# Weights times values on quarters of the array: two partial sums in two banks, one pair of heads a step

## The chip, the cores and the metric

The kernel runs on one core of one Trainium2 chip. The metric is the device time of one execution in microseconds (us). The core has TensorE (PE; its weight loads are shown apart as PEld), VectorE (DVE), ScalarE (ACT), GpSimd (POOL) and SyncE (SP), each with its own queue, worked off in order; they wait for each other by semaphores. TensorE writes to PSUM, which has eight banks of 2 KB per partition.

## What is computed

Attention whose scores are mixed across the 12 heads before the softmax and whose weights are mixed across the heads after it, and behind it two expert layers, all in float32 (batch 2, 12 heads, 448 tokens, 64 per head):

```python
def _attn_ref(q, k, v, w_pre, w_post):
    scale = 1.0 / np.sqrt(q.shape[-1])
    scores = scale * np.matmul(q, k.transpose(0, 1, 3, 2))
    scores = np.einsum('bhij,hg->bgij', scores, w_pre)
    scores = scores - np.max(scores, axis=-1, keepdims=True)
    attn = np.exp(scores)
    attn = attn / (np.sum(attn, axis=-1, keepdims=True) + 1e-09)
    attn = np.einsum('bhij,hg->bgij', attn, w_post)
    return np.matmul(attn, v)
...
x = _moe_ref(x, w_gate, w_val, w_out)    # (silu(x wg) * (x wv)) wo
x = _moe2_ref(x, w_in, w_out)            # (h * relu6(h + 3) / 6) w2o with h = x w2i
```

## The kernel before

The 896 query tokens are cut into 8 tiles t of up to 120 tokens, four for each batch entry, and each tile into 9 to 12 chunks of 10 tokens (90 chunks). Two chunks make one step i of the main loop (45 steps); in the 128 partitions of a chunk lie heads times tokens, which makes the mix over heads a matmul.

For each pair of heads c of a tile, `scores` (L166, tile name pqk) multiplies queries and keys on quarters of the array (64 rows by 64 columns) into two banks, and `scores_out` (L182) copies them to S: the even head on VectorE, the odd one on ScalarE. `relayout` (SP) and `relayout_rest` (GpSimd, L206) move S by DMA into the order of chunks, sx. `premix` (L217, ppre) mixes the heads; `row_max` (L230, VectorE), `exps` (L236, ScalarE) and `weights` (L242 and L243 on VectorE, L245 on GpSimd, wn) prepare the softmax; the division goes into wn, a copy of w_post for each row. `postmix` (L259, ppost) multiplies with wn and brings the keys to the partitions. `attn_out` (L283) copies its two banks to the tile at: the first on VectorE, the second on ScalarE.

When a tile is complete, `av` (L295, pav) multiplies its weights with the values, a pair of heads c at a time, on 128 rows (keys) by 64 columns (one head each), in one bank. `x_out` (L313) copies that bank on VectorE to a staging tile xs, which `x_split` on GpSimd later splits into two float32r parts (xh, xl). For the last two tiles `x_last` (L333 ScalarE, L334 VectorE) does that straight from the bank.

The order of a step i is written out by hand. TensorE: postmix(i), scores of the pairs due in that step, premix(i + 2), in the last three steps some matmuls of the first expert product (`fill`), then av of the pairs due. ScalarE: the exponentials for step i + 1, the second bank of attn_out, the second score copy. VectorE: the first bank of attn_out, the reciprocals of the first chunk of step i + 1, the first score copy, the reciprocals of the second chunk, two maxima, then x_out. Tables give each pair its step: a tile's scores lie in the steps ahead of its first premix (those of tiles 2 to 7 end in steps 7, 13, 17, 24, 29 and 35), and av of tile t lies behind the tile's last postmix, two pairs in each of three steps. The expert weights of the first two products are converted in steps 24 to 27 and 32 to 35.

The PSUM tags are pqk (2 banks; scores and av), ppre (4) and ppost (2). Behind step 44 and the rest of `fill`, av of tile 7 runs for all six pairs with ppre and ppost in turn, and then the expert products, which take TensorE to the end.

## Time and profile before

| | us |
|---|---|
| median of three runs | 717.46 (711.99 to 725.30) |
| the profiled execution | 713.29 |
| its span, first to last instruction | 711.5 |
| TensorE, MATMUL records | 685.4 (96%) |
| VectorE | 503.4 (71%) |
| ScalarE | 296.9 (42%) |
| GpSimd | 176.5 (25%) |

Busy times come from one profiled execution. The ends of matmuls are modelled, so records overlap and a busy TensorE is not one at its peak; how long a block takes is read from its start to the next block's start. A float32 matmul shows as two records.

### The profile page before, as it was taken

How to read it: one execution, taken by the hardware profiler on the slowest of the kernel's cores; microseconds unless marked ns; L12 is line 12 of the kernel's file. 1: busy time of each engine (PE TensorE's matmuls, PEld its weight loads, DVE VectorE, ACT ScalarE, POOL GpSimd, SP SyncE). 2: the span in 40 equal slices, each digit the busy share in tenths (PEclk: the TensorE clock that was granted, in tenths of full speed). 3: DMA queues.
4: the chain of work that ended last, by engine and by line, in shares of the span. 5: the costliest groups of instructions: out<-in, count | busy, mean ns of one | idle time of the engine just before them, and what ended most of it. 6: DMA issues, size and time to landing. Idle time of an engine off the chain costs nothing.

```text
span 711.5 us, 16611 instructions
## 1 busy us (share of the span) xinstructions
PE 685.4 (96%) x6864; PEld 571.6 (80%) x6864; DVE 503.4 (71%) x853; ACT 296.9 (42%) x563; POOL 176.5 (25%) x275
## 2 busy tenths in 40 slices
PE   9699899799899999999999999999999999999997
PEld 3355565465579999999999999999999999999997
DVE  4676677688745888888888665668888888765550
ACT  4565466456543433434343322334445544333320
POOL 2444265454640221131112000002332332000000
PEclk9999999899999999999999999999999999999999
DMA  5777456443421424323242334232323323544420
GB/s 198 225 204 202 134 138 180 136 145 84 132 92 46 134 89 133 121 101 130 93 131 92 119 106 132 89 92 92 127 89 96 127 82 100 162 145 145 136 72 27
DMA packets 33629, 86.75 MB, mean 122 GB/s; under 512 B 9264, under 2 KB 21952, under 8 KB 33552
## 3 DMA queue, kind: packets, MB, share of 16 engines
q1 hardware_dynamic: 25632, 80.97, 35.3%
q0 software_dynamic: 7200, 3.94, 2.8%
q8 instruction: 54, 0.88, 0.5%
q10 hardware_dynamic: 720, 0.77, 0.3%
q14 instruction: 23, 0.19, 0.1%
HBM read 62.20 MB, written 2.75 MB: 91 GB/s over the span
## 4 chain that ended last, share of the span: by engine, by line
PE 87%; DMA 5%; issue 2%; DVE 2%; ACT 2%; POOL 1%; SPq 0%; POOLq 0%; ACTq 0%
PE pi L394 16%; PE pp L394 16%; PE po L394 12%; PE pg L394 12%; PE pv L394 12%; PE ppost L259 5%; PE pav L295 5%; PE pqk L166 4%; PE ppre L217 3%; DMA sx<-S 3%; DMA k<-in_k_dram 1%; PE p L394 1%; ACT e L236 1%; DMA q<-in_q_dram 1%; POOL wn L245 1%
## 5 line engine op out<-in xcount | busy, mean ns | idle before, releaser
L394 PE MATMUL pp<-g,hp 128*128 128x448 f32 x384 | 109.1, 365 | 0.0
L605 POOL TENSOR_TENSOR g<-rl,g 128x448 fp32r<-128x448 f32 x32 | 41.5, 1318 | 168.5 <-ACT g L604 168.5
L394 PE MATMUL po<-u,ho 128*128 128x448 f32 x288 | 81.7, 364 | 0.0
L236 ACT ACTIVATE e<-ppre,nm 128x448 f32<-128x448 f32 x90 | 56.4, 631 | 52.8 <-DVE nm L230 52.7
L259 PEld LDWEIGHTS ppost<-wn,e 60*64 60x64 f32 x2880 | 49.5, 137 | 34.3 <-POOL wn L245 29.7
L394 PEld LDWEIGHTS pp<-g,hp 128*128 128x128 f32 x384 | 72.0, 187 | 5.8
L605 POOL TENSOR_TENSOR u<-sg,u 128x448 fp32r<-128x448 f32 x24 | 32.9, 1391 | 151.2 <-ACT u L604 151.2
L394 PE MATMUL pi<-x2h,li 128*128 128x448 f32 x192 | 70.2, 366 | 0.0
L394 PE MATMUL pi<-x2l,hi 128*128 128x448 f32 x192 | 70.0, 364 | 0.0
L394 PE MATMUL pi<-x2h,hi 128*128 128x448 f32 x192 | 69.9, 364 | 0.0
L394 PE MATMUL pp<-g,lp 128*128 128x448 f32 x192 | 69.3, 361 | 0.0
L259 PE MATMUL ppost<-wn,e 60*64 60x60 f32 x2880 | 56.1, 224 | 12.5 <-POOL wn L245 11.3
L206 POOL DMA_DIRECT2D sx<-S x90 | 54.5, 606 | 33.9 <-issue 11.0
L230 DVE TENSOR_REDUCE nm<-ppre 128x1 f32<-128x448 f32 x90 | 51.7, 613 | 12.7 <-PE ppre L217 12.0
L394 PEld LDWEIGHTS po<-u,ho 128*128 128x128 f32 x288 | 54.1, 188 | 3.8
L217 PE MATMUL ppre<-sx,W 64*64 64x448 f32 x360 | 51.1, 558 | 4.6 <-DMA sx<-S 4.6
L166 PE MATMUL pqk<-k,q 64*64 64x448 f32 (+4 forms) x384 | 51.5, 570 | 2.6 <-ACT S L182 2.0
L394 PE MATMUL po<-u,lo 128*128 128x448 f32 x144 | 52.3, 363 | 0.0
L394 PE MATMUL pg<-xl,hg 128*128 128x448 f32 x138 | 50.5, 366 | 0.0
L394 PE MATMUL pv<-xl,hv 128*128 128x448 f32 x138 | 50.5, 366 | 0.0
L394 PE MATMUL pg<-xh,hg 128*128 128x448 f32 x138 | 50.5, 366 | 0.0
L295 PEld LDWEIGHTS pav<-at,v 128*64 128x64 f32 x768 | 36.9, 137 | 16.9 <-ACT S L182 11.8
(105 smaller groups left out, 1369.3 us busy)
## 6 DMA issues: line engine op xcount, KB each, us to landing
sx<-S SPq DMA_DIRECT2D x90, 182.0 KB
ri<-in_moe_w_in_dram SPq DMA_DIRECT2D x16, 768.0 KB
rg<-in_moe_w_gate_dram SPq DMA_DIRECT2D x12, 768.0 KB
rv<-in_moe_w_val_dram SPq DMA_DIRECT2D x12, 768.0 KB
ro<-in_moe_w_out_dram SPq DMA_DIRECT2D x12, 768.0 KB
rp<-in_moe_w_out_dram SPq DMA_DIRECT2D x12, 640.0 KB
rp<-in_moe_w_out_dram SPq DMA_DIRECT2D x6, 768.0 KB
sx<-S POOLq DMA_DIRECT2D x90, 42.0 KB, 4.9
```

The source lines that it names most:

```text
L166: nc.tensor.matmul(p[e][lo:hi, :S], lhsT=qs[b][r, base + lo : base + hi], rhs=ks[b][r, c, :], start=True, stop=True, tile_position=(64 * e ...
L206: nc.gpsimd.dma_start(out=sx[m // 2][104:128, m % 2, :], in_=rows[8:, :H, :])
L217: nc.tensor.matmul(p[a][64 * r : 64 * r + 64, :S], lhsT=W1[rows, :], rhs=x[rows, r, :], start=True, stop=True, tile_position=(64 * a, 64 * r),
L230: nc.vector.tensor_reduce(nm, pre[m][:, :S], AX.X, ALU.max, negate=True)
L236: nc.scalar.activation(e[:, :S], pre.pop(m)[:, :S], AF.Exp, bias=tot.pop(m), scale=1.0, accum_out=sm)
L245: nc.gpsimd.tensor_scalar(wn, W2, rc, 1.0, ALU.mult, ALU.mult)
L259: nc.tensor.matmul(p[s][64 * c : 64 * c + 64, r, b, :, :], lhsT=e[rows, k0 : k0 + 64], rhs=wn[rows, :, :], start=True, stop=True, tile_pos ...
L295: nc.tensor.matmul(p[64 * e : 64 * e + 64, :n], lhsT=vs[b][:, jc, h, :], rhs=ats[t][:, jc, h, :n], start=jc == 0, stop=jc == JC - 1, tile_ ...
L394: nc.tensor.matmul(p[:, :S], lhsT=wt[:, kk, :], rhs=xx, start=start, stop=stop)
L605: eng.tensor_tensor(to[1], src, to[0].bitcast(F32), ALU.subtract)
```

## The change

`av` uses quarters of the array as scores, premix and postmix do. The 128 rows of keys are cut into two halves of 64; each half accumulates in a bank of its own (p[0] and p[1]), so that a pair of heads is 16 matmuls on 64 rows by 64 columns instead of 8 on 128 by 64. `add_halves` brings the two banks together on the way out: a ScalarE copy of the first, then a VectorE add of the second. In x_out this stands in the place of the VectorE copy; in x_last it is put ahead of the cast and the subtraction, with a new tile xl.

The table of steps is changed too: a tile's pairs are spread one to a step where the steps suffice (two in steps 18, 20, 23 and 40) instead of two in every second or third. `attn_out` is cut in two: its second bank, on ScalarE, is now copied behind the step's scores and score copies. From step 43 on av takes banks of ppre, and at the end each pair of tile 7 takes two banks of ppre or two of ppost.

```diff
-    def av(t, c, tag="pqk"):
+    def av(t, c, tags=("pqk", "pqk")):
...
-        p = ps.tile([128, 512], F32, name=f"pav{t}_{c}", tag=tag, bufs=BUFS[tag])
+        p = [ps.tile([128, 512], F32, name=f"pav{t}_{c}_{r}", tag=tags[r], bufs=BUFS[tags[r]]) for r in range(2)]
         for jc in range(JC):
-            for e in range(2):
-                h = 2 * c + e
-                nc.tensor.matmul(
-                    p[64 * e : 64 * e + 64, :n],
-                    lhsT=vs[b][:, jc, h, :],
-                    rhs=ats[t][:, jc, h, :n],
-                    start=jc == 0,
-                    stop=jc == JC - 1,
-                    tile_position=(0, 64 * e),
-                )
+            for r in range(2):
+                for e in range(2):
+                    h = 2 * c + e
+                    nc.tensor.matmul(
+                        p[r][64 * e : 64 * e + 64, :n],
+                        lhsT=vs[b][64 * r : 64 * r + 64, jc, h, :],
+                        rhs=ats[t][64 * r : 64 * r + 64, jc, h, :n],
+                        start=jc == 0,
+                        stop=jc == JC - 1,
+                        tile_position=(64 * r, 64 * e),
+                    )
...
-        nc.vector.tensor_copy(stage[t][:, c, :n], pavs.pop((t, c))[:, :n])
+        add_halves(stage[t][:, c, :n], pavs.pop((t, c)), n)
+
+    def add_halves(out, p, n):
+        nc.scalar.copy(out, p[0][:, :n])
+        nc.vector.tensor_tensor(out, out, p[1][:, :n], ALU.add)
...
-        p = pavs.pop((t, c))[:, :n]
+        x = pe.tile([128, 120], F32, name=f"xl{t}_{c}", tag="xl", bufs=4)
+        p = x[:, :n]
+        add_halves(p, pavs.pop((t, c)), n)
...
-            i = begin + (c // 2) * (end - begin) // 2
-            at_step(i, av, t, c, place="av")
+            i = begin + c * (end - begin + 1) // HP
+            at_step(i, av, t, c, ("pqk" if i < NP - 2 else "ppre",) * 2, place="av")
...
         if i >= 0:
-            attn_out(i)
+            attn_out(i, 0)
         for m in soft[:1]:
             weights(m)
         run(i, "qk")
+        if i >= 0:
+            attn_out(i, 1)
...
-        av(7, c, ("ppre", "ppost")[c % 2])
+        av(7, c, (("ppre", "ppre"), ("ppost", "ppost"))[c % 2])
```

In VectorE's order at the end of step 14 (tile 1's pairs 2 and 3 in the kernel before) stand, before:

```order
L230 TENSOR_REDUCE nm32_1495<-ppre16_0_1489 128x1
L230 TENSOR_REDUCE nm33_1497<-ppre16_1_1490 128x1
L313 COPY xs1_1334<-pav1_2_1499 128x120
L313 COPY xs1_1334<-pav1_3_1508 128x120
L283 COPY at2_1285<-ppost15_0_1528 128x2x48x5
```

and now:

```order
L230 TENSOR_REDUCE nm32_1575<-ppre16_0_1569 128x1
L230 TENSOR_REDUCE nm33_1577<-ppre16_1_1570 128x1
L316 TENSOR_TENSOR xs1_1394<-xs1_1394,pav1_2_1_1580 128x120
L281 COPY at2_1345<-ppost15_0_1608 128x2x48x5
L242 TENSOR_SCALAR rc32_1647<-sm32_1642 128x1
```

Two copies out of the banks of pairs 2 and 3 have become one add for pair 2, of its second bank (pav1_2_1); pair 3 has moved into step 15.

In ScalarE's order the exponentials for step 16 (e2, e3) and what follows them in step 15 stand, before:

```order
L236 ACTIVATE e2_113,sm32_1562<-ppre16_0_1489,nm32_1495 128x448
L236 ACTIVATE e3_114,sm33_1564<-ppre16_1_1490,nm33_1497 128x448
L283 COPY at2_1285<-ppost15_1_1529 128x2x48x5
L182 COPY S0_107<-pqk4_3_1_1574 110x448
L236 ACTIVATE e4_115,sm34_1635<-ppre17_0_1586,nm34_1592 128x448
```

and now:

```order
L315 COPY xs1_1394<-pav1_2_0_1579 128x120
L236 ACTIVATE e2_113,sm32_1642<-ppre16_0_1569,nm32_1575 128x448
L236 ACTIVATE e3_114,sm33_1644<-ppre16_1_1570,nm33_1577 128x448
L182 COPY S0_107<-pqk4_3_1_1653 110x448
L281 COPY at2_1345<-ppost15_1_1609 128x2x48x5
L315 COPY xs1_1394<-pav1_3_0_1676 128x120
L236 ACTIVATE e4_115,sm34_1735<-ppre17_0_1666,nm34_1672 128x448
```

The score copy stands ahead of the at copy now, and the copy of the pair's first bank stands ahead of the exponentials of the next step.

## Rows read from the trace of the kernel before

**Rows 1.** Busy us by stretch; columns: stretch, length, engines' busy (instructions), clock, DMA.

```profile
43.26:219.06 175.80, 161.29 (x3853) 102.81 (x3852) 118.81 (x354) 95.80 (x238) 84.46 (x173) 0.98 0.47 137
219.06:711.50 492.44, 488.72 (x2414) 452.61 (x2412) 359.72 (x433) 179.03 (x274) 74.42 (x56) 1.00 0.34 109
```

**Rows 2.** The same view, 43.26 to 219.06 cut; engines: PE, PEld, DVE, ACT, POOL.

```profile
43.26:55.17 11.91, 11.79 (x274) 6.47 (x273) 8.74 (x26) 7.17 (x18) 4.27 (x10) 1.00 0.65 186
55.17:65.04 9.87, 9.37 (x197) 4.94 (x193) 6.85 (x20) 4.90 (x12) 4.89 (x11) 1.00 0.66 195
65.04:75.84 10.80, 10.80 (x224) 6.19 (x224) 7.07 (x21) 5.80 (x15) 4.57 (x11) 1.00 0.79 198
75.84:98.28 22.44, 20.02 (x483) 11.56 (x481) 15.80 (x46) 12.91 (x33) 9.93 (x22) 1.00 0.36 118
98.28:121.56 23.28, 22.86 (x602) 14.95 (x600) 17.66 (x55) 13.90 (x36) 14.26 (x30) 1.00 0.68 190
121.56:165.19 43.63, 36.68 (x859) 21.98 (x857) 29.88 (x86) 24.08 (x57) 21.29 (x45) 0.92 0.46 135
165.19:188.30 23.11, 20.54 (x552) 12.93 (x553) 18.61 (x56) 13.49 (x33) 10.92 (x25) 1.00 0.32 93
188.30:219.06 30.76, 29.23 (x676) 23.78 (x676) 14.19 (x48) 13.56 (x37) 14.33 (x25) 1.00 0.25 85
```

**Rows 3.** TensorE in order of time: start, us, line, out<-in, [idle before <-releaser].

```profile
66.02 1.79 PE L166 MATMUL pqk<-k,q 64*64 64x448 f32 x8
67.74 0.98 PE L217 MATMUL ppre<-sx,W 64*64 64x448 f32 x8
...
101.91 1.16 PE L259 MATMUL ppost<-wn,e 60*64 60x60 f32 x64
102.89 0.93 PE L166 MATMUL pqk<-k,q 64*64 64x448 f32 x8
103.65 0.93 PE L217 MATMUL ppre<-sx,W 64*64 64x448 f32 x8
104.50 1.89 PE L295 MATMUL pav<-at,v 128*64 128x120 f32 x32
106.32 1.16 PE L259 MATMUL ppost<-wn,e 60*64 60x60 f32 x64
```

**Rows 4.** Groups by line and shape, 43.26 to 219.06: busy us, mean ns | idle before.

```profile
L230 DVE TENSOR_REDUCE nm<-ppre 128x1 f32<-128x448 f32 x76 | 43.7, 613 | 8.3 <-PE ppre L217 7.7
L283 DVE COPY at<-ppost 128x480 f32<-128x480 f32 x39 | 26.3, 675 | 19.9 <-PE ppost L259 19.8
L182 DVE COPY S<-pqk 120x448 f32<-120x448 f32 x14 | 8.5, 609 | 3.0 <-PE ppre L217 1.9 <-DMA sx<-S 0.6 <-PE pqk L166 0.5
L334 DVE TENSOR_TENSOR xl<-pav,xh 128x120 fp32r<-128x120 f32 x6 | 1.7, 281 | 5.5 <-ACT xh L333 5.5
L333 ACT CAST xh<-pav 128x120 fp32r<-128x120 f32 x6 | 1.6, 260 | 6.6 <-PE pav L295 6.6
```

**Rows 5.** The chain that ended last, from 54 to 67 us: start, us, what.

```profile
56.55 6.85 DMA k<-in_k_dram
63.40 0.63 POOL sx L206
```

**Rows 6.** TensorE in order of time, waits at the tile changes.

```profile
136.97 2.64 PE L217 MATMUL ppre<-sx,W 64*64 64x448 f32 x6 [3.03 <-DMA sx<-S]
...
183.92 1.16 PE L259 MATMUL ppost<-wn,e 60*64 60x60 f32 x64 [1.53 <-POOL wn L245]
```

**Rows 7.** All engines in order of time, steps 44 and the tail.

```profile
210.05 1.04 PE L295 MATMUL pav<-at,v 128*64 128x120 f32 x16 [0.68 <-DVE xl L334]
...
214.87 4.26 PE L295 MATMUL pav<-at,v 128*64 128x98 f32 x96
215.81 0.24 ACT L333 CAST xh<-pav 128x98 fp32r<-128x98 f32 x1 [4.42 <-PE pav L295]
216.09 0.26 DVE L334 TENSOR_TENSOR xl<-pav,xh 128x98 fp32r<-128x98 f32 x1 [4.37 <-ACT xh L333]
```

More of the change, by code (lines that the diff above doesn't have):

```diff
@@ L267, in postmix, with attn_out @@
         post[i] = p
-    def attn_out(i):
-        p = post.pop(i)
-        (t0, c0), (t1, c1) = chunks[2 * i], chunks[2 * i + 1]
-        for t, c in ((t0, c0), (t1, c1)):
-            if c == 0:
-                ats[t] = pat.tile([128, JC, H, 120], F32, name=f"at{t}", tag="at")
-        for r in range(2):
-            if t0 == t1:
-                dst = ats[t0][:, :, :, c0 * KI : (c0 + 2) * KI].rearrange("p b h (a k) -> p a (b h) k", k=KI)
-                dst = dst[:, :, :, r * KG : (r + 1) * KG]
-            else:
-                t, c = chunks[2 * i + r]
-                dst = ats[t][:, :, :, c * KI : (c + 1) * KI].rearrange("p b h (a k) -> p a (b h) k", k=KG)
-            copy = nc.scalar.copy if r else nc.vector.tensor_copy
-            copy(dst, p[r].rearrange("p a b h k -> p a (b h) k"))
+    def attn_out(i, r):
+        p = post[i][r]
+        (t0, _), (t1, _) = chunks[2 * i], chunks[2 * i + 1]
+        t, c = chunks[2 * i + r]
+        if c == 0:
+            ats[t] = pat.tile([128, JC, H, 120], F32, name=f"at{t}", tag="at")
+        if t0 == t1:
+            dst = ats[t][:, :, :, (c - r) * KI : (c - r + 2) * KI].rearrange("p b h (a k) -> p a (b h) k", k=KI)
+            dst = dst[:, :, :, r * KG : (r + 1) * KG]
+        else:
+            dst = ats[t][:, :, :, c * KI : (c + 1) * KI].rearrange("p b h (a k) -> p a (b h) k", k=KG)
+        copy = nc.scalar.copy if r else nc.vector.tensor_copy
+        copy(dst, p.rearrange("p a b h k -> p a (b h) k"))
```

## The prediction

> **What bounds the kernel now.** I read the busy time by stretch first. From 219.06 us to the end of the span (711.5) the matmuls of the two expert layers keep TensorE at 488.7 of 492.4 us, and nothing that the change touches lies there. So the change can only act before 219.06, and as the first block of weights times values starts in step 6, on the 175.8 us from 43.26 on, where TensorE is busy 161.3 us [rows 1]. Next the same 175.8 us cut at starts of a postmix (one starts each step; the one cut at 55.17 lies at a block of weights times values) [rows 2]: in three of them TensorE misses over 2 us. Last the order of time on TensorE [rows 3]. A step runs postmix (ppost), scores (pqk), premix (ppre) and in some steps a block of two pairs of heads (pav x32). One full step goes from 101.91 to 106.32, 4.41 us: 0.98 + 0.76 + 0.85 + 1.82. With tile 3, whose second score group has 26 columns, pqk takes 1.72 instead of 0.76 (66.02 to 67.74).
>
> **The matmuls of weights times values.** Before, a pair of heads is 8 matmuls on 128 rows by 64 columns, two side by side; now it is 16 on 64 by 64, four side by side. Each matmul shows as two records. No row shows this form, so I bound it by its neighbours on quarters [rows 3]. pqk: 8 records in 0.76 us are two rounds of four, 0.38 us for 448 columns. ppost: 64 records in 0.98 are 16 rounds, 0.061 us for 60 columns. In proportion to pqk a round of 120 columns takes 0.102 us, on the straight line through both 0.110; eight rounds are 0.81 to 0.88 us a pair. The block of 96 records before takes 4.26 us for 48 rounds of 98 columns with its entry and exit, 0.089 each [rows 7], where 0.083 is the proportional value and 0.092 the line's; so I take 0.82, near the proportional end. A block of two pairs costs 1.82 + 0.09 now (the 0.09 is the premix ahead of it, which needs 0.85 where scores need 0.76), against 2 x 0.82: about 0.27 to 0.3 us for going from quarters to halves of the array and back. There are 21 such blocks in steps 6 to 43, so some 6 us of TensorE time go away; by 0.88 a pair it would be 3 us.
>
> The Trainium skill ("TensorEngine Tiling (Array Packing)", Performance Considerations, Instruction Overhead) speaks against this: every matmul carries about 60 cycles of overhead, so cutting matmuls up gains nothing where they are already short. By that page the 384 added matmuls would cost, as an estimate, 384 x 25 ns = 9.6 us, and the sum below would end 3 us above the time before instead of 7 below. The trace does not agree where the form is nearest: the ppost round of four matmul records takes 61 ns in all.
>
> **Evening out.** Steps without a block end in waits, steps with one don't. After the change a full step is 0.98 + 0.76 + 0.76 + 0.82 = 3.32 us of TensorE (4.28 with tile 3), 2.56 without scores. I set this against each stretch [rows 2]:
> - 43.26 to 55.17 (steps 6, 7, half of 8): 2 x 3.32 + 3.46 = 10.1 against 11.9: -1.8.
> - 55.17 to 65.04: the chain of waits [rows 5] goes through a key transfer of 6.85 us and then GpSimd's issue of the relayout, not through TensorE: 0.
> - 65.04 to 75.84 (steps 11, 12): 2 x 4.28 = 8.6 against 10.8: -2.2.
> - 75.84 to 98.28 (13 to 17): 5.8 + 4 x 3.32 = 19.1 against 22.4, but step 13's three score groups still wait for each other's copies (1.3) and tile 3's relayout is only just in time (0.8): -1.2.
> - 98.28 to 121.56 (18 to 23): 20.4 of TensorE; steps 18, 20 and 23 get two pairs, and the second pair waits for the banks of the first (below, 0.75 each): -0.5.
> - 121.56 to 165.19 (24 to 32): it waits for the relayouts of tiles 5 and 6 (the longest time 3.03 us, on a premix) [rows 6]. Their start hangs on the step in which the tile's last scores are copied, so shorter steps behind it only lengthen the wait. Only steps 27 to 29 count: -1.3.
> - 165.19 to 188.30 (33 to 38): the same for tile 7 (1.53 us on wn, held up behind GpSimd's relayout) [rows 6], and VectorE already has 18.6 of 23.1 us: 0.
> - 188.30 to 219.06: steps 39 to 43 -1.1; step 44, where the second pair waited 0.68 us for its bank [rows 7] and one pair moves to step 43, -1.7; the tail +1.3 (below): -1.5.
>
> Together -8.5.
>
> **The way out of the banks.** Before, one VectorE copy empties a pair's bank. Now a ScalarE copy of about 260 ns and then a VectorE add of about 281 ns do, one after the other, by x_last's cast and subtraction of the same shape [rows 4]: 48 more ScalarE operations, 12.5 us, and 12 more on VectorE in the pairs that are written by x_last. In a full step they are hidden. The pair ends 0.82 us after the premix; the copy is done at 1.1, the add waits behind the two maxima (2 x 613 ns) and is done near 1.5; the next scores want the banks at 0.82 + 0.94 = 1.76. If that cover of 0.25 us is gone, each us of delay is a us of TensorE. With two pairs in a step it is gone: the second pair can start at 1.55 instead of 0.82, 0.75 us in each of the three steps above. Queued behind the waiting ScalarE copy are the next step's exponentials: they start at 1.1 instead of 0.7, end at 2.4, and their reciprocal waits in any case until VectorE has copied the scores at 3.2. So that costs nothing unless VectorE's order slips.
>
> ScalarE's at copy moves behind its score copy; I take both as long as VectorE's, 675 and 609 ns [rows 4]. Its bank is wanted by the next postmix 1.6 us after the scores end, the two copies need 1.3: hidden by premix and the new pair. The score copies come one at copy earlier on ScalarE but not on VectorE (at copy, first reciprocal, score copy), and the pair needs both banks: gain 0, and as the pair now comes right behind the premix I add 0.06 us a step for 25 steps, +1.5.
>
> In the tail each pair runs copy, add, cast, subtract. The links are 0.28 us (215.81 to 216.09) [rows 7], so ScalarE comes round every 0.77 us against 0.71 a pair on TensorE, and the first matmuls on hf=1 need a ppost bank that the last copy frees: about +0.9, and +0.4 for the casts in steps 40 to 42 that hold up exponentials.
>
> **Sum.** -8.5 + 1.5 = -7.0 us on the profiled execution's 713.3 us (its span 711.5 and 1.8 around it), 706.3. The median of the three runs, 717.5, is 4.2 higher; the same change there gives 710.5. Between them I forecast 708.
>
> **Rivals.**
> 1. The copies out of PSUM set the step. VectorE is busy 18.6 us in the six steps of 165.19 to 188.30 [rows 2], 3.1 a step; three of them copy no scores, and with a score copy (609 ns) in each it would be 3.4, above TensorE's 3.32. If that can't overlap and some 0.3 us of waiting joins it, a full step takes 3.7, and 0.4 us for about 20 steps eats the gain: 714. For it: those six steps. Against it: they hold the conversion of expert weights too, which other steps don't. The Trainium skill (same page, PSUM Bottleneck) has the rule: tiling speeds up TensorE and not the emptying of PSUM.
> 2. The DMA waits shrink too. Of TensorE's 14.5 us missing from 161.3 to 175.8 [rows 1] half would go: -14, 701. For it: earlier score copies on ScalarE start some relayouts earlier. Against it: VectorE's copy of the other head is as late as before.
> 3. ScalarE's wait is on the path. Its copy holds the exponentials 0.43 us in each of the 39 steps from 6 on; the reciprocals then come late, GpSimd's wn too, and postmix waits. Fully on the path that is 17 us: 17 - 7 = +10, 725. It decides from 0.2 us a step on (7 us / 39). Against it: 0.8 us of slack at the score copy.
> 4. A stall near the tile changes grows past the 3 us of 136.97 and TensorE falls to 1.2 GHz behind it, as in the stretch 121.56 to 165.19, whose granted clock is 0.92 [rows 2]: 8% of 43.6 us is 3.5 us of lost clock. One more such fall takes half of the gain, 710 to 712.
> 5. Each of the 384 added matmuls carries a fixed time: from 18 ns on it eats the 7 us, 714 to 716. Against it: of ppost's 61 ns round the line leaves 12 ns as fixed, for four records.
>
> **Chances.** My forecast without a fall (702 to 710): 0.40, with one, rival 4 (710 to 713): 0.13. Rival 1 (713 to 720): 0.19. Rival 5 (the same): 0.03. Rival 2 (below 702): 0.13. Rival 3: 0.12, of which 0.03 beyond 731. Three runs of the kernel before lie 13 us apart, so the measured time may fall anywhere some 5 us around these. A change of 2% (14 us) is about what a measurement here can tell from none. Faster by over 2% (below 703): 0.17; within 2%: 0.79; slower: 0.04. The range of 8 in 10 runs from 698 (rival 2 with its error) to 722 (rival 3 in part); the forecast's own is 702 to 713.
>
> **What the profile of the changed kernel would show.** If right: pairs as x32 records of 64x64 in 0.8 to 0.85 us to the next start, and no 0.85 behind a premix; full steps of 3.3 to 3.5 us; waits for wn gone from steps between 6 and 23, but premixes still waiting for sx at tiles 5, 6 and 7, the longest over 3.03. If rival 1: TensorE waiting on the add or on score copies in most steps, VectorE above 85%. If rival 3: postmix waiting for wn in most steps, with ScalarE's exponentials right behind the new copy. I am wrong if the stretch 43 to 219 shrinks by less than 3 us or more than 14, or if the rest of the span moves by more than 1.

## The result: slower by half a per cent

| | before | after |
|---|---|---|
| median, us | 716.09 (711.99 to 725.30, 20 runs) | 719.51 (716.17 to 724.33, 20 runs) |
| the profiled execution, us | 713.29 | 719.34 |
| its span | 711.5 | 717.6 |

The ratio after to before is 1.0052, 95% interval 1.0031 to 1.0074. The forecast was 708 us, so its sign was wrong: instead of 7 us less, the profiled execution takes 6.05 us more. By the medians it is 3.4 us: the profiled execution before lies 2.8 us below its median, the one after at its median. So nearly half of what the views below divide up is the spread of single executions, and 1 to 2 us in one stretch are no finding by themselves.

The busy time of the page after:

```profile
PE 687.9 (96%) x7632; PEld 582.9 (81%) x7632; DVE 507.9 (71%) x865; ACT 304.8 (42%) x611; POOL 176.7 (25%) x275
```

The same view as [rows 1] and [rows 2], cut where the steps 6, 8, 11, 13, 18, 24, 33 and 39 start and where the expert products begin (stretch, length, then busy us of PE, PEld, DVE, ACT, POOL with their instructions, granted clock, DMA):

```profile
44.33:52.63 8.30, 7.75 (x222) 5.76 (x224) 6.29 (x19) 5.00 (x13) 3.71 (x9) 1.00 0.69 188
52.63:66.15 13.52, 13.15 (x343) 7.22 (x342) 8.99 (x27) 7.72 (x21) 5.73 (x13) 1.00 0.62 181
66.15:76.42 10.27, 9.46 (x232) 5.06 (x228) 6.21 (x19) 5.15 (x14) 3.68 (x8) 1.00 0.74 206
76.42:99.03 22.61, 20.88 (x583) 13.36 (x579) 16.20 (x49) 13.94 (x37) 9.54 (x22) 1.00 0.36 117
99.03:126.03 27.00, 24.38 (x737) 17.49 (x733) 18.27 (x56) 15.51 (x43) 15.83 (x31) 1.00 0.61 172
126.03:168.33 42.30, 36.66 (x1027) 23.97 (x1019) 29.66 (x86) 24.28 (x65) 20.84 (x44) 0.96 0.45 137
168.33:193.51 25.18, 21.63 (x654) 15.87 (x650) 18.97 (x56) 14.83 (x40) 11.64 (x27) 0.93 0.34 96
193.51:225.12 31.61, 29.56 (x882) 24.85 (x876) 18.11 (x59) 16.97 (x53) 13.60 (x23) 1.00 0.22 75
225.12:717.60 492.48, 488.71 (x2412) 452.62 (x2412) 360.21 (x435) 179.02 (x274) 74.43 (x56) 1.00 0.33 109
```

The expert products begin at 225.12 instead of 219.06 and then take 492.48 us against 492.44 [rows 1]: all of the loss lies ahead of them, as the prediction said that any effect would. By stretch, each against the same steps before:

| steps | 0 to 5 | 6, 7 | 8 to 10 | 11, 12 | 13 to 17 | 18 to 23 | 24 to 32 | 33 to 38 | 39 to the end |
|---|---|---|---|---|---|---|---|---|---|
| change, us | +1.1 | +0.3 | -0.3 | -0.5 | +0.2 | +3.7 | -1.3 | +2.1 | +0.8 |

Of steps 24 to 32 the first three and the last five take as long as before, to 0.1 us; the change lies in step 27, before and after:

```profile
139.10:144.93 5.83, 5.83 (x113) 4.40 (x113) 4.84 (x12) 3.20 (x8) 3.38 (x8) 0.68 0.36 91
143.59:147.96 4.37, 4.37 (x122) 3.50 (x119) 3.33 (x10) 2.56 (x7) 1.81 (x5) 0.76 0.40 110
```

Steps 0 to 5, ahead of the first pair, show how wide the spread of single executions is: in the runs below they lie between 3.1 us less and 4.1 us more than before.

TensorE's order of time shows two things at once (start, us, line, out<-in, [idle before <-releaser]). First the end of step 8, which has scores of tile 3 and one pair; this answers to [rows 3]:

```profile
55.33 0.98 PE L217 MATMUL ppre<-sx,W 64*64 64x448 f32 x8
56.13 1.01 PE L294 MATMUL pav<-at,v 64*64 64x120 f32 x32
56.95 1.20 PE L259 MATMUL ppost<-wn,e 60*64 60x60 f32 x62
```

A pair of 32 records goes from its start to the next start in 0.82 us (56.13 to 56.95), and the premix ahead of it in 0.80 (55.33 to 56.13). The price of the pair and the end of the switch between halves and quarters are as predicted. Then step 18, one of the four with two pairs:

```profile
100.71 1.11 PE L294 MATMUL pav<-at,v 64*64 64x120 f32 x32
102.10 0.42 PE L294 MATMUL pav<-at,v 64*64 64x120 f32 x4 [0.28 <-ACT xs L315]
102.80 0.94 PE L294 MATMUL pav<-at,v 64*64 64x120 f32 x26 [0.27 <-DVE xs L316]
```

The second pair starts 1.39 us after the first, when ScalarE has copied the first bank; it runs the 4 records that this bank allows and then stands until VectorE's add has freed the second: together 2.77 us to the next postmix (103.48) for what is 1.64 us of matmuls, and the old block of two pairs took 1.82 [rows 3].

All that TensorE waited for between 43 and 219 us in the kernel before (engine, line, <- what; us in total, times, longest):

```profile
PE ppost L259 <- POOL wn L245: 5.5, 9, 1.5
PE ppre L217 <- DMA sx<-S: 4.6, 3, 3.0
PE pqk L166 <- ACT S L182: 2.0, 3, 0.7
PE pav L295 <- ACT S L182: 0.8, 4, 0.2
PE pav L295 <- DVE xl L334: 0.7, 1, 0.7
```

and the largest sums after:

```profile
PE ppre L217 <- DMA sx<-S: 5.6, 3, 3.6
PE pqk L166 <- ACT S L182: 2.0, 3, 0.7
PE ppost L259 <- issue: 1.8, 4, 0.6
PE ppost L259 <- POOL wn L245: 1.6, 3, 1.1
PE pav L294 <- DVE rc L242: 1.3, 4, 0.4
PE pav L294 <- ACT xs L315: 0.9, 3, 0.4
PE ppre L217 <- issue: 0.8, 1, 0.8
...
```

The waits for wn shrink from 5.5 to 1.6 us. In their place stand the pair's own: for VectorE (rc L242 comes right behind the score copy there, which frees the bank) and for the copy of the first bank. "Issue" means that the trace shows nothing that was waited for; the kernel before has none of it in this stretch, and it comes back below.

The tail answers to [rows 7]:

```profile
220.02 4.78 PE L294 MATMUL pav<-at,v 64*64 64x98 f32 x192
225.12 0.47 PE L399 MATMUL pg<-xh,hg 128*128 128x448 f32 x1 [0.33 <-ACT xl L315]
```

It takes 5.10 us from the first pair to the first product, 4.19 before.

### The profile page after: what moved, and what is told of

Read it like the earlier page. It is cut to its first block, busy times and chain, and to the rows that moved or that the text cites. A ratio compares the mean times of both kernels' runs of the same rounds, so it can differ in the third digit from the quotient of the medians.

```text
span 717.6 us, 18253 instructions
## 1 busy us (share of the span) xinstructions
PE 687.9 (96%) x7632; PEld 582.9 (81%) x7632; DVE 507.9 (71%) x865; ACT 304.8 (42%) x611; POOL 176.7 (25%) x275
## 4 chain that ended last, share of the span: by engine, by line
PE 86%; DMA 5%; ACT 2%; DVE 2%; issue 2%; SPq 1%; POOL 1%; ACTq 0%; POOLq 0%; DVEq 0%
PE pi L399 16%; PE pp L399 16%; PE po L399 12%; PE pg L399 12%; PE pv L399 12%; DMA sx<-S 5%; PE pav L294 5%; PE pqk L166 4%; PE ppost L259 4%; PE ppre L217 3%; SPq L199 1%; ACT e L236 1%; PE p L399 1%; DVE S L182 1%; DVE nm L230 0%
## 5 line engine op out<-in xcount | busy, mean ns | idle before, releaser
L259 PEld LDWEIGHTS ppost<-wn,e 60*64 60x64 f32 x2880 | 54.4, 136 | 19.0 <-POOL wn L245 11.6
L259 PE MATMUL ppost<-wn,e 60*64 60x60 f32 x2880 | 59.3, 222 | 9.9 <-POOL wn L245 4.6
L294 PEld LDWEIGHTS pav<-at,v 64*64 64x64 f32 x1536 | 46.8, 135 | 26.7 <-ACT S L182 15.8
L294 PE MATMUL pav<-at,v 64*64 64x120 f32 (+3 forms) x1536 | 57.1, 265 | 3.8 <-DVE rc L242 1.3
L217 PE MATMUL ppre<-sx,W 64*64 64x448 f32 x360 | 54.4, 559 | 6.4 <-DMA sx<-S 5.6
```

The lines of the kernel that those rows point to most:

```text
L217: nc.tensor.matmul(p[a][64 * r : 64 * r + 64, :S], lhsT=W1[rows, :], rhs=x[rows, r, :], start=True, stop=True, tile_position=(64 * a, 64 * r),
L259: nc.tensor.matmul(p[s][64 * c : 64 * c + 64, r, b, :, :], lhsT=e[rows, k0 : k0 + 64], rhs=wn[rows, :, :], start=True, stop=True, tile_pos ...
L294: nc.tensor.matmul(p[r][64 * e : 64 * e + 64, :n], lhsT=vs[b][64 * r : 64 * r + 64, jc, h, :], rhs=ats[t][64 * r : 64 * r + 64, jc, h, :n] ...
```

## Experiments

Theory A says that the way out of the two banks (a copy, then an add, and banks that scores and pairs share) costs what quarters save. Theory B says that the saved time was never there, because the steps are held by something other than TensorE's matmuls. Ratios are against the kernel before, measured on the same chip in the same series.

### One part alone

> The quarters and the two-bank exit alone: two pairs in every second or third step as before, and attn_out in its old place. Theory A (the way out of the banks loses the time): the second pair of each of the 21 blocks waits about 0.7 us for the first pair's copy and add, +14 us, against 6 us less switching on TensorE: 5 to 9 us slower than the kernel before. Theory B (the new table of steps loses it): the quarters alone gain, 3 to 6 us faster than before. Theory C (the split of attn_out loses it): also 0 to 6 us faster than before.

```diff
-            i = begin + c * (end - begin + 1) // HP
+            i = begin + (c // 2) * (end - begin) // 2
...
             attn_out(i, 0)
+            attn_out(i, 1)
```

(against the changed kernel: the old table and the old place of the second at copy.) Measured: 728.06 us, ratio 1.0143 (1.0114 to 1.0172). With two pairs in every such step the waits of step 18 stand in all of them:

```profile
PE pav L294 <- ACT xs L315: 5.3, 18, 0.4
```

In the 21 steps with two pairs, a second pair starts some 0.6 us later on the mean than the first one's matmuls take, some 13 us in all (the row holds only what shows as idle). So theory A is right for two pairs in a step.

> The kernel before with the new table alone: one pair a step, on halves of the array, one bank, one VectorE copy. TensorE now changes from quarters to halves in 39 steps and not 21: at 0.3 us each +5 us. Theory A: the evening out gains about as much, so 0 to 5 us faster or the same as before (-5 to +2 us). Theory B: slower than before by 4 us or more. Theory C: the same as A.

```diff
-            i = begin + (c // 2) * (end - begin) // 2
+            i = begin + c * (end - begin + 1) // HP
```

(against the kernel before) 716.66 us, 0.9990 (0.9961 to 1.0019).

> The kernel before with attn_out cut in two alone: ScalarE's at copy behind the score copies. Theories A and B: within 1.5 us of the kernel before, since the next postmix wants that bank later and VectorE's score copy is as late as before. Theory C: 3 us or more slower, with TensorE's postmix waiting for the at copy.

```diff
-            attn_out(i)
+            attn_out(i, 0)
...
         run(i, "qk")
+        if i >= 0:
+            attn_out(i, 1)
```

715.00 us, 0.9982 (0.9958 to 1.0006).

> The kernel before with the new table and the cut attn_out together, on halves of the array and one bank a pair. If the two only add up: -0.7 and -1.3 us, 1 to 3 us faster than the kernel before. If the spread needs the earlier score copies to work: 4 us or more faster. If they hinder each other: the same or slower.

Both of these edits together, with the pairs still on halves in one bank: 717.26 us, 0.9987 (0.9959 to 1.0016). The table and the split at copy neither gain nor lose by themselves; they only serve to win back most of the 10 us that quarters lose without them (1.0143 in e1, 1.0052 with them).

### The four doubled steps

> The changed kernel, but the pairs of the four doubled steps (18, 20, 23, 40) in the old form: halves of the array, one bank each, one VectorE copy. Theory A1 (the second pair's wait for copy and add): in the changed kernel these waits are 1.0 to 1.1 us in each of the four steps, against some 0.3 us of switching that comes back: 2.5 to 3.5 us faster than the changed kernel, so 0 to 2 us slower than the kernel before. Theory A2 (the exit costs a little in every step, through ScalarE's or VectorE's queue): within 1 us of the changed kernel, 3 to 5 us slower than before. Theory A3 (what is saved is lost again at the relayouts): the same as A2.

```diff
+            if i in (18, 20, 23, 40):
+                at_step(i, av_whole, t, c, place="av")
```

(av_whole is the old av: halves of the array, one bank, a VectorE copy.) Measured: 716.23 us, 0.9986 (0.9961 to 1.0011), that is some 4.7 us (0.66%) less than the changed kernel; steps 18 to 23 are +0.8 us against the kernel before instead of +3.7. By the medians the four doubled steps are all of the loss. But what is left is no gain either: 40 pairs still run on quarters, and the time equals that of the kernel before.

### The order of the copies, and their engine

> The changed kernel with the reciprocals of the first chunk put behind the scores and their copies, so that VectorE copies the scores about 0.3 us earlier in a step. In the changed kernel the pair starts 0.15 to 0.25 us late in nearly every full step, after the score copies. If that wait is worth its length on the path (some 25 steps): 4 to 6 us faster than the changed kernel, so 0 to 3 us faster than the kernel before. If the steps are held elsewhere (copy and add behind the pair, GpSimd, the relayouts): as the changed kernel, 2 to 5 us slower than the kernel before, and the wait shows up behind the pair instead.

```diff
             attn_out(i, 0)
-        for m in soft[:1]:
-            weights(m)
         run(i, "qk")
...
-        for m in soft[1:]:
+        for m in soft:
             weights(m)
```

721.27 us, 1.0060 (1.0037 to 1.0083). Nothing is gained. The pair still starts as late behind a premix (0.92 us by the median of the steps with scores and one pair, where a premix takes 0.76; 0.945 in the changed kernel). Only its waits for VectorE's score copy (rc L242) fall, from 1.3 to 0.2 us in all; in their place TensorE's waits for wn grow from 1.6 to 3.6 us, since both reciprocals come later.

> The changed kernel with as many operations on the way out, but without the chain: ScalarE copies the first bank, VectorE copies the second one to a scrap tile, and neither waits for the other; the sum of the halves is left out. Theory A1: the second pair of a doubled step waits for the copies only and, as VectorE's comes behind its two maxima as before, still waits 0.5 to 0.7 us; ScalarE's wait for the add in steps 40 to 44 is gone: 1 to 2 us faster than the changed kernel. Theory A2 by the chain: 3 us or more faster than the changed kernel. If the operations as such cost, not their chain: within 1 us of the changed kernel.

```diff
-        nc.vector.tensor_tensor(out, out, p[1][:, :n], ALU.add)
+        nc.vector.tensor_copy(scrap[:, :n], p[1][:, :n])
```

(against the changed kernel; the sum of the halves is left out) 720.99 us, 1.0043 (1.0019 to 1.0067): 0.6 us less than the changed kernel by the ratios, give or take some 2.4 us by the two intervals. A chain that costs 3 us or more is not there.

> The changed kernel with both operations of the exit on VectorE, a copy and an add; ScalarE's queue is as before the change. Theory A2 by ScalarE's queue (the copy holds the exponentials): 3 us or more faster than the changed kernel. Theory A2 by VectorE's queue (its step of 3.1 to 3.4 us is the bound): 48 x 0.28 = 13 us more of it, 5 to 12 us slower than the changed kernel. Theories A1 and A3: 0 to 4 us slower.

```diff
-        nc.scalar.copy(out, p[0][:, :n])
+        nc.vector.tensor_copy(out, p[0][:, :n])
```

724.96 us, 1.0110 (1.0077 to 1.0143): with ScalarE's queue relieved and VectorE's 13 us fuller it is 4 us worse than the changed kernel. The edit does both at once, so by itself it doesn't settle rival 3 (ScalarE's exponentials queued behind the new copy). What speaks against rival 3 is its own sign: postmix should wait for wn in most steps, and these waits fell from 5.5 to 1.6 us (3 times).

### Is TensorE the limit of these steps?

> The kernel before with half of the matmuls of weights times values left out (two of the four groups of keys; the other half of the sum is missing). 41 pairs in steps 6 to 43 lose 0.41 us of TensorE each, 16.8 us, and the last seven 2.5 us. If TensorE's time is what the steps end on (my prediction's reckoning): 12 to 19 us faster than the kernel before. If most of it only turns into waits, for the score copies, wn and the relayouts: 3 to 8 us faster, 2.5 of these in the tail.

```diff
-        for jc in range(JC):
+        for jc in range(2):
...
-                    stop=jc == JC - 1,
+                    stop=jc == 1,
```

(against the kernel before; two of the four groups of keys are left out) 706.53 us, 0.9865 (0.9824 to 0.9905), some 9.7 us less. A block of two pairs falls from 1.79 to 0.97 us (1.36 to 0.76 in tile 3, 1.66 to 0.90 in tile 4): the 21 blocks of steps 6 to 44 lose 16.4 us of TensorE time, and the tail is 2.0 shorter. In its trace steps 6 to 38 hold 13.1 us less of matmuls and are only 3.9 us shorter. By the median about half of the time taken off TensorE reaches the end ((9.7 - 2.0) of 16.4, by the interval 0.3 to 0.65 of it), by the trace three tenths (the profiled execution before is a short one). It is spread unevenly: steps 6 to 12 are 2.9 us shorter for 3.3 taken off (steps 11 and 12 by all of 1.64), steps 13 to 38 only 1.0 us for 9.8. So theory B holds for the kernel before, above all from step 13 on: a us off TensorE is not a us off the step.

> The kernel before with GpSimd's first two relayouts of a tile issued in the step of the tile's last scores, not one step later. If the waits at the tile changes hang on that issue: the waits of 3.0 us (tile 5) and those at tiles 6 and 7 shrink by up to one step each, 3 to 8 us faster than the kernel before. If GpSimd's issues only hold up wn earlier, or the transfers themselves are the limit: within 2 us.

```diff
-        while rests < placed and rests // 2 <= i + LOOK + 3 and i > scored[chunks[rests][0]]:
+        left_now = 2
+        while rests < placed and rests // 2 <= i + LOOK + 3 and (
+            i > scored[chunks[rests][0]] or (i == scored[chunks[rests][0]] and left_now > 0)
+        ):
             relayout_rest(rests)
             rests += 1
+            left_now -= 1
```

705.94 us, 0.9869 (0.9827 to 0.9911). In its trace steps 24 to 32 are 8.1 us shorter, without one change to TensorE's work. TensorE's waits from 120 to 160 us there:

```profile
PE ppost L259 <- issue: 1.5, 1, 1.5
PE ppost L259 <- POOL wn L245: 1.0, 2, 0.7
PE pqk L166 <- ACT S L182: 0.7, 1, 0.7
...
```

and the windows of the same kernel (columns as above):

```profile
121.00:160.00 39.00, 35.01 (x931) 21.39 (x932) 30.23 (x87) 24.94 (x60) 22.38 (x47) 1.00 0.50 152
```

The wait of premix for sx (3.03 us in [rows 6]) is gone, and the granted clock is 1.00 where the kernel before had 0.92 [rows 2]: the wait itself and the low clock behind it both went. Of the edits that leave every matmul in place this is the only one with a large gain.

> The changed kernel with the first two relayouts that GpSimd issues for a tile one step earlier, as in e10 on the kernel before. If the anchor at the tile changes and the change are independent: -9.4 us as there, ratio 0.990 to 0.994. If the early relayouts take away the waits behind which the change's own losses lay: 0.994 to 1.000.

The same edit on the changed kernel: 711.61 us, 0.9908 (0.9873 to 0.9944). From 1.0052 to 0.9908 is 1.4%, against 1.3% for the same edit on the kernel before: the relayout wait and the loss by quarters are separate.

> Quarters in single steps and halves in doubled ones, with the same earlier relayouts. If the relayouts are what eats the 6 us that quarters save on TensorE: 5 us or more faster than the kernel before, and more than the earlier relayouts bring by themselves. If not: the sum of the two, 0 to 3 us faster than before.

The same edit on the version with the four doubled steps in the old form: 706.87 us, 0.9882 (0.9843 to 0.9920), not told apart from e10. Even with the doubled steps and the relayout waits gone, quarters bring nothing that shows.

> Quarters only where x_out empties the banks in single steps; the doubled steps, tile 6 and tile 7 in the old form, so that copy, add, cast and subtract never follow each other on ScalarE and VectorE. In single executions steps 39 to the end are 1.3 us longer than before with quarters there and 1.3 to 2 us shorter with the new table on halves. If that is the long chain of x_last: 1.5 to 3.5 us faster than the hybrid, 2 to 5 us faster than the kernel before. If not: as the hybrid, 0 to 2 us faster than before.

```diff
-            if i in (18, 20, 23, 40):
+            if i in (18, 20, 23) or t == 6:
...
-        av(7, c, (("ppre", "ppre"), ("ppost", "ppost"))[c % 2])
+        av_whole(7, c, ("ppre", "ppost")[c % 2])
```

(against e5) 718.86 us, 1.0036 (1.0002 to 1.0070): not faster than e5, so the longer chain of x_last in tiles 6 and 7 is not what is missing. Why it is 0.5% slower than e5 stays open; its one trace has more "issue" time than any other (12.7 us, below).

### What holds a full step at 3.5 us

An undisturbed step with scores and one pair takes 3.45 to 3.6 us after, where the predicted sum was 3.32. Step 29 shows what stands in it (in order of time; postmix starts at 151.85 and the next at 155.36):

```profile
153.54 1.08 PE L217 MATMUL ppre<-sx,W 64*64 64x448 f32 x8
...
153.97 0.53 ACT L182 COPY S<-pqk 120x448 f32<-120x448 f32 x1 [0.34 <-PE pqk L166]
154.01 0.60 DVE L182 COPY S<-pqk 120x448 f32<-120x448 f32 x1
...
154.55 0.79 PEld L294 LDWEIGHTS pav<-at,v 64*64 64x64 f32 x30 [0.70 <-ACT S L182]
```

Scores, their copies, the pair and its way out follow one another on the same two banks. Both score copies start as soon as the scores have ended, some 0.4 us into the premix, and the pair starts with the end of the first of them, 1.01 us behind the premix, which alone takes 0.76. Two theories: this ring sets the step, or the softmax chain from premix to postmix does.

> The changed kernel with another order in each step: TensorE postmix, pair of heads, premix, scores (instead of postmix, scores, premix, pair); VectorE and ScalarE take the pair's way out of the banks right behind the at copies, then the softmax of the next step, and the score copies last. Loop theory (postmix, at copy, reciprocal, score copy, pair, next postmix hold a full step at 3.5 us and not TensorE's 3.3): the pair no longer waits for the score copy, full steps come to 3.3 us, 4 to 7 us less than the changed kernel, 0.990 to 0.996 of the kernel before. Rival, the softmax chain from premix to postmix holds the steps: premix is later in its step by the pair, nothing gained or up to 6 us lost, 1.005 to 1.013. Second rival, only the doubled steps and the tile changes count: 1.003 to 1.007.

```diff
             attn_out(i, 0)
+        for k, (f, args) in enumerate(extra[i]["av"]):
+            f(*args)
+            g, gargs = extra[i]["exit"][k]
+            g(*gargs)
         if i >= 0:
             attn_out(i, 1)
...
-        run(i, "av")
+        run(i, "qk")
```

724.75 us, 1.0099 (1.0063 to 1.0134). The pair's second bank now waits for the score copy of the step before: in one step the first 4 records start at 153.05 and the others from 153.42 on. The order only moves the wait.

> The version with four doubled steps in the old form and with the first two relayouts of GpSimd a step earlier (e11), with the same order postmix, pair, premix, scores. If the loop through the score copy is what kept e11 at the time of e10: 2 to 6 us below e10, ratio 0.979 to 0.985 to the kernel before. If the steps are held by the softmax chain: the same as e10 and e11 (0.987) or up to 6 us worse.

> The kernel before with the new table, the split at copies, the early relayouts and the order postmix, pair, premix, scores, but pairs on halves of the array in one bank. It separates the order from the quarters: if the order alone helps, it stands 1 to 4 us below e10 (0.981 to 0.986) and quarters (e14) add at most 3 us more; if quarters need this order to bring anything, it is not below e10 (0.987 to 0.992) while e14 is.

The same order on top of e11 gives 708.30 us, 0.9868 (0.9815 to 0.9922), and with the pairs on halves in one bank 707.45 us, 0.9848 (0.9802 to 0.9894): both as e10 within the intervals. The order theory falls; it didn't separate the ring from the softmax chain, as both orders keep the ring.

> The changed kernel, every instruction in the same place on every engine, but PSUM dealt out anew: two banks that only the pairs use, two for the scores, two for postmix and two (instead of four) for premix. Bank theory (a step that has scores and a pair holds the same two banks four times in turn: scores, their copy out, pair, its way out, and that ring sets the step): waits of the pair for the score copy and of the scores for the add go away, full steps come from 3.5 to 3.3 us, stretches of steps 11 to 18 and 33 to 39 shorten by 1 to 2 us each, 4 to 8 us less than the changed kernel in all, 0.992 to 0.998. Rival, softmax chain or VectorE's order hold the step: TensorE waits elsewhere, same as the changed kernel, 1.003 to 1.008. Second rival: premix with two banks waits for the exponentials, up to 0.3 us in each step, 1.010 to 1.020.

```diff
-    BUFS = {"pqk": 2, "ppre": 4, "ppost": 2}
+    BUFS = {"pqk": 2, "ppre": 2, "pav": 2, "ppost": 2}
...
-            at_step(i, av, t, c, ("pqk" if i < NP - 2 else "ppre",) * 2, place="av")
+            at_step(i, av, t, c, ("pav", "pav"), place="av")
```

720.26 us, 1.0044 (1.0013 to 1.0076); no instruction moved on any engine. TensorE in order of time, step 14 of this kernel:

```profile
84.79 1.14 PE L259 MATMUL ppost<-wn,e 60*64 60x60 f32 x64
85.72 0.97 PE L166 MATMUL pqk<-k,q 64*64 64x448 f32 x8
86.48 1.08 PE L217 MATMUL ppre<-sx,W 64*64 64x448 f32 x8
87.23 1.05 PE L294 MATMUL pav<-at,v 64*64 64x120 f32 x29
88.05 0.21 PE L259 MATMUL ppost<-wn,e 60*64 60x60 f32 x1
```

3.26 us, with 0.93 + 0.76 + 0.75 + 0.82 and no wait. Steps 19 and 21 take 3.28, and each of steps 9 to 12 (tile 3) 4.27: the predicted 3.32 and 4.28. So the ring over the shared banks is what held a full step at 3.5 us, and the step that the prediction added up exists. Yet the whole is as slow as the changed kernel. Steps 6 to 41, with the same matmuls in them, take 161.3 us here and 159.5 us after (155.0 before): the waits changed places. In its trace steps 11 to 17 are 3.2 us shorter than before, and steps 24 to 32 3.3 us; steps 18 to 23 (+4.1), 33 to 38 (+2.7), 6 and 7 (+4.9) and 39 to the end (+2.5) are longer.

> The version with the four doubled steps in the old form and the early relayouts (e11, 0.988) with the same new dealing of the banks. Bank theory: the saved TensorE time shows at last, 3 to 6 us below e10, 0.978 to 0.983. Rival, softmax chain or VectorE's order: as e10 and e11, 0.986 to 0.990. Second rival, premix waits for its two banks: above e11, 0.992 to 1.005.

The same banks with the doubled steps in the old form and the early relayouts: 710.24 us, 0.9906 (0.9864 to 0.9948), no better than e10 or e11. Its profiled execution took 705.8 us, the fastest of its eight; there steps 6 to 17 are 4.2 us shorter than before, of which steps 18 to 23 (+1.0) and 39 to the end (+1.7) give back 2.7.

### Where the rest may go: TensorE's code

In e17 the largest new wait, 3.34 us in step 7, has no releaser. It and its surroundings in order of time:

```profile
46.38 0.37 PE L259 MATMUL ppost<-wn,e 60*64 60x60 f32 x7
...
47.91 0.21 ACT L236 ACTIVATION_READ_ACCUMULATOR e<-ppre,nm 128x1 f32 x1
50.09 0.38 PE L259 MATMUL ppost<-wn,e 60*64 60x60 f32 x5 [3.34 <-issue]
```

TensorE stops in the middle of a postmix whose operands are there. The stop costs more than its idle time: step 7, in which it lies, takes 9.62 us at a granted clock of 0.65, step 6 took 3.31 at 1.00:

```profile
43.01:46.32 3.31, 3.31 (x111) 2.75 (x115) 2.74 (x9) 2.42 (x6) 1.89 (x5) 1.00 0.57 180
46.32:55.94 9.62, 6.28 (x125) 4.51 (x119) 3.68 (x11) 2.57 (x7) 2.01 (x5) 0.65 0.54 157
```

Between 47.29 and 48.55 us the trace has one packet of the instruction queue q8, and none else between 40.27 and 52.13. Its row in the DMA view of 47.25 to 48.6 us, beside the data queue's (packets, MB, share of 16 engines):

```profile
q1 hardware_dynamic: 161, 0.26, 71.8%
...
q8 instruction: 1, 0.02, 5.8%
```

The other large ones are alike. In e17 TensorE resumes at 109.36 and 174.02, 1.31 and 1.41 us after the ends of such packets; in e5 at 54.01, 60.92 and 205.12, 1.45, 1.46 and 1.53 us after; in the changed kernel at 48.92, 62.75, 70.59, 95.95 and 118.43, 1.33 to 1.44 us after. Taken over the traces of both kernels and all 18 runs, all 84 waits that are put down to "issue" between 43 and 219 us end 1.20 to 1.64 us after the end of such a packet; of the 369 waits with another releaser 24 do. The stops also stand at the ends of equal pieces of code: in the changed kernel 257 records of PE and PEld lie from 62.75 to 70.59, 1282 from there to 95.95 and 1282 again to 118.43, which is 1.00, 5.01 and 5.01 times 256. What makes a packet come late is open. It doesn't take a busy data queue: in e4's stop of 2.61 us it took 1.5% of the DMA engines around the packet (209.7 to 210.8 us), in e12's of 2.70 us 8.0% (211.3 to 212.5). The page has 60 such packets for 7632 matmul and as many load records, 254 records a packet, and 54 before for 6864 (0.98 and 0.88 MB). The idle time of TensorE put down to "issue" between 43 and 219 us is, in one profiled execution each:

| pairs on halves | us | pairs on quarters | us |
|---|---|---|---|
| before | 0 | after | 2.9 |
| e2, e3, e8 | 1.6, 1.6, 1.3 | e1, e4, e5 | 1.0, 6.9, 7.7 |
| e9 | 0.9 | e6, e7, e11 | 5.1, 2.6, 5.3 |
| e10 | 2.6 | e12, e13, e14 | 12.7, 7.7, 5.0 |
| e16 | 5.2 | e15, e17, e18 | 6.8, 7.2, 2.8 |
| mean | 1.9 | mean | 5.7 |

In the version with the doubled steps in the old form (e5) it is the largest sum of all of TensorE's waits from 43 to 219 us:

```profile
PE ppost L259 <- issue: 7.4, 7, 2.9
```

A pair on quarters is 64 records (32 matmuls, 32 loads) where it was 32, and a step in which TensorE waits less works through its code faster. Both fit that it stands for its code more often: on the mean 3.8 us more in the quarters' versions, though single executions lie far apart (0.9 to 12.7 us, on halves 0 to 5.2). That is of the size of what e5 and e11 lack: 34 of their pairs in steps 6 to 44 are on quarters, each (1.82 + 0.09) / 2 - 0.82 = 0.135 us shorter than before, 4.6 us together. The reading is by times and counts of the traces; no run changed the code's size alone, so that this is the whole of the missing part is not shown.

## Why the prediction was wrong, step by step

- **The place.** Right: the expert layers moved by 0.04 us.
- **The matmuls.** Right to the hundredth: 0.82 us a pair, and no switch behind premix. The Trainium skill's objection ("TensorEngine Tiling (Array Packing)", Instruction Overhead: some 60 cycles for each matmul) is not what the trace shows: a pair takes the 0.82 us that were put for its eight rounds of 120 columns, without the 8 x 25 ns that the estimate by that page would add; rival 5 fell. What more matmuls did bring is more code, a term that the sum lacked. (The 21 old blocks lie in steps 6 to 44, not 43.)
- **Evening out.** This is the step that failed. It set TensorE's matmuls (3.32 us) against each stretch as if nothing else could end a step, and took -1.8, -2.2 and -1.2 in steps 6 to 17. Measured are 0, -0.5 and +0.2. e9 shows the error without any quarters: of 13.1 us taken off TensorE in steps 6 to 38 3.9 came through, and from step 13 on a tenth. e17 shows what the 3.32 needed: banks that scores and pairs don't share. With them steps 13 to 17 are 0.9 us shorter than before (e17) and 1.4 (e18), where 1.2 was put. For steps 11 and 12 the reckoning was right and the one trace unlucky: in e5, e6, e11 and e15, whose pairs there are the changed kernel's, these steps are 2.1 to 2.2 us shorter, as put; in the changed kernel's trace the stop at 70.59 (0.81 us, "issue") lies in step 11, which took 5.87 us against 4.29 in e5.
- **Doubled steps.** The mechanism was right (the second pair waits for the banks of the first), the size wrong: -0.5 was put for steps 18 to 23, +3.7 was measured. The second pair was to run from 1.55 us after the first on; in step 18 its first 4 records start at 1.39 and the rest at 2.09, since the add comes half a us later than put. So step 18 needs 2.77 us for two pairs where the old block needed 1.82. The rest stands in the steps between: the pair of step 19 takes 1.53, waiting for the score copy, and postmix takes 1.43 in step 19 and 1.72 in step 22 (0.51 of it an "issue" wait), where 0.95 is undisturbed. And step 40, also doubled, was priced without a wait.
- **The score copy.** The cover of 0.25 us for the scores held: they follow postmix in 0.93 to 0.99 us in most steps. The wait on the other side of the ring was mis-sized. Behind a premix the pair comes 4.2 us later over 22 steps with scores and one pair (a premix that waits for sx left out), 0.19 each, where 0.06 was put. In 17 of these steps the pair starts 0.05 us after the end of ScalarE's score copy, which had begun as soon as the scores ended in nearly all of them: the copy takes longer than what is left of the one premix that now lies between scores and pair. In steps 28, 30 and 34 the pair stands another 0.5 to 0.7 us between its first and its second bank; there VectorE's score copy comes late, behind its at copy.
- **24 to 32.** The number came out (-1.3 put and measured), and so did the wait on sx (3.59 us where "over 3.03" was said); the way there did only in part, so the number is half luck. Steps 28 and 29 are 0.5 us longer, not shorter, and all of the 1.3 lies in step 27 (5.83 us before, 4.37 after): one pair less stands there (0.66 us instead of 1.36), and the granted clock is 0.76 instead of 0.68 (the two rows above), with scores in 0.88 us instead of 1.50. e10 shows the anchor: not the steps but the turn of GpSimd's relayout holds this stretch, 8 us of it.
- **33 to 38.** 0 put, +2.1 measured. Premix waited 1.53 us for tile 7's sx, where it had been 0.6, and the granted clock of the stretch is 0.93 where it was 1.00 [rows 2]: 0.07 x 25.18 = 1.8 us of clock. This does not come in every execution: with the same pairs there the stretch is 0.1 us shorter than before in e5, equal in e7 and 1.6 longer in e6.
- **The tail.** +0.9 put, +0.91 measured (5.10 against 4.19 us). Of the -2.8 for steps 39 to 44 the -1.7 for step 44 came (8.52 us from its postmix to the tail's first pair, 10.26 before). The -1.1 for steps 39 to 43 became +1.7 (17.99 against 16.31 us): step 40 is doubled, and step 43's first matmuls of the fill wait for their operand (0.5 us).
- **The account.** Between the -7.0 that was put and the +6.05 of the profiled execution lie 13.05 us: 4.9 in steps 6 to 17, 4.2 in steps 18 to 23, 2.1 in 33 to 38, 2.3 from 39 to the end and 1.1 in steps 0 to 5, less the 1.5 that the sum had put apart for the score copies. Steps 6 to 17, 18 to 23 and 39 to the end come short of what was put in most of the runs with these pairs too; what steps 0 to 5 and 33 to 38 lost lies within the spread of single executions.
- **The rivals.** Rival 1 named the outcome (713 to 720) and the Trainium skill's PSUM Bottleneck (the same page: packing speeds up TensorE and leaves the emptying of PSUM as it was) stood beside it; by e1 and e5 it is the larger part of the truth, though by the ring of two banks and not by VectorE's busy share, which is 71% as before. Rivals 2, 3 and 5 fell. Rival 4 came and was paid back: the new low clock in 33 to 38 costs 1.8 us, and 24 to 32 has 0.96 now where the nearly same stretch had 0.92 [rows 2], 0.04 x 42.30 = 1.7 us less.

## What to carry to other kernels

Before a stretch is reckoned by its busiest engine, find out what a us taken off that engine brings; leaving out half of the matmuls in question tells it in one run, stretch by stretch. Price a change that cuts matmuls by the ring on its banks too (write, copy out, write, copy out), with each copy in its engine's turn, and let no two such users follow each other on the same banks (here that brought the step to its sum, though not yet the kernel). Look for the stretch whose wait sets the time, here the turn of one DMA issue (1.3% for moving two issues by one step), before speeding up what lies between such waits.

## What the runs showed of the hardware that was not expected

TensorE can wait for its own code: it stops at pieces of 256 records and resumes 1.20 to 1.64 us after a 16 KB packet of its instruction queue has ended (84 of 84 such waits here), having stood for up to 3.69 us (e13, at 53.91). The data queues can be busy in the packet's time (72% in e17) or nearly idle (1.5% in e4). Such a wait has no releaser in the trace and is put down to "issue"; behind some of the longest the granted clock was at the lower of its two levels for a while (0.65 over step 7 of e17). On the mean of the single traces here the versions with many small matmuls have more of it (5.7 against 1.9 us).

Neighbouring blocks on quarters run into each other. In the changed kernel postmix starts at 103.48 while the last two records of the pair start at 103.57, so a step's blocks are told apart by their first records, not by their last.
